# Chunk-selected attention and top-1 experts: head pairs in one written order for all engines, transposes in two visits, half the scores on two column tiles, bounds without the first query tile

## The chip, the cores and the metric

The kernel runs on one core of a Trainium2 chip. A core has five engines with instruction streams of their own: TensorE (PE; its weight loads are shown as PEld), VectorE (DVE), ScalarE (ACT), GpSimd (POOL) and SyncE (SP), which here only issues DMAs. They meet through semaphores, and each works its own stream in order. Matmuls write to PSUM[...]; DVE and ACT read PSUM[...]. The metric is device time in microseconds; the median of the runs before is 374.56.

## The reference

Attention over 4 batches, 8 heads, 768 positions and 64 columns per head, in which each query sees only 6 chunks of 32 keys, picked by an upper bound of its scores; then a mixture of 8 experts, of which each token takes one.

```python
ub = sum(maximum(q * k_min, q * k_max), axis=-1)      # per query and chunk of 32 keys
ub = where(causal, ub, -1e9)
top_chunks = argsort(ub)[..., -6:]
scores = where(sel & (pos_q >= pos_k), q @ k.T / 8, -1e9)
attn = exp(scores - max); attn = attn / (sum(attn) + 1e-9)
x = attn @ v                                          # 3072 tokens of 512
logits = x @ w_gate; e = argmax(logits); g = softmax(logits)[e]
out = g * (relu(x @ w1[e]) @ w2[e])
```

A query of the first 128 positions has at most four causal chunks, so its selection of six takes all of them.

## The kernel before

Work goes by pairs of heads: 16 pairs, four per batch (pair i: batch i // 4, `hp` = i % 4). The two heads fill the 128 partitions where both are needed, 64 each.

*Preparation of a pair* (`prep_steps`). `k_half` transposes three tiles of keys into a `ps_m` tile; DVE reduces it to largest and smallest value of each chunk, ACT copies the two heads, scaled by 1/8, to `KTE`. `q_t` and `q_e` do so for queries: DVE copies the transposed tile to `qT`, ACT writes its absolute value to `qA` and copies the second head to `QSB`; POOL copies the first head (in `late`, run by `flush`). `kse` forms sum and difference of largest and smallest on DVE, in `KS` and `KD`. `ub` multiplies them with `qT` and `qA`: q.(max + min) + |q|.(max - min) ranks chunks as the reference's bound does. ACT copies that to `ubT`, `select` transposes it, DVE adds the causal bias, finds the eight largest per row with MAX8 and marks every chunk below the sixth (`nsel`); `mask` transposes the marks, and ACT writes them as 24 further rows of `QSB`. `KTE` has -50 in the rows for each chunk's keys, so that the score matmul itself adds -50 for a chunk that is not selected.

*Attention of a pair.* Seven units of scores (`units`): units 0 and 1 for the first 384 queries, 2 to 6 for the second. `scores(i, u)` multiplies on TensorE (bf16, keys as columns of the array) into a `ps_s` tile, ACT takes Exp into `P`, POOL zeroes the part above the diagonal with affine_select where keys and queries meet (units 0, 1, 5, 6). `attend(i, u)` multiplies v with `P` (f32, the two heads on two column tiles of the array) into `po`, and DVE adds `P` to a running sum `acc`; at the end of a half DVE copies `po` to `ot`.

*Router steps of a pair* (`router_steps`). `ud` sums `acc` over the keys and multiplies `ot` with the gate on four column tiles; `lgp` transposes the result, DVE takes reciprocals and scales the logits, POOL adds them up (`sums`); `xr` transposes `ot` and writes the token rows to `xrow`. Per batch `route_steps` has `logits` (eleven DVE operations and an Exp on ACT), `rank` (counts on TensorE, five DVE operations) and `scatter` (POOL writes token rows to the expert's place in DRAM by indirect DMA, 128 rows each).

*Experts.* 31 tiles of 128 tokens at most, of which 28 run always: `gather`, `x_in` (a DMA transpose), `meta`, `up` (matmul, Relu, DMA transpose), `down` (matmul, scaling, indirect DMA to the output). Which expert a tile has is worked out by `table`, first for eleven tiles that three batches fill (19 DVE operations), then for the rest. The weights are loaded in 32 pieces by POOL (`load_w`), spread over the attention.

*Order.* TensorE, POOL and SP follow the order of the program. DVE and ACT do so in `first_pair` and from the last pair on; in between a scheduler places their instructions. The loop over pairs goes through four groups of units; with group g of pair i run the bounds and selection of pair i + 1, the keys and queries of pair i + 2, and router steps of pair i - 1. `first_pair` prepares pair 0 step by step, with spinning matmuls[...].

*Buffers.* PSUM: three banks in `ps_m` (transposes, bounds, masks, router), two tiles of two banks in `ps_s` (scores), one bank in `ps_o` (`po`).

Of the kernel before, what the change touches and what calls it, by code (L numbers as in the profile page):

```python
# [24 lines left out]
def kernel(  # L25
# [52 lines left out]
    cbias = const.tile([128, 3, 2, NCH], FP32)  # L78
    thr = const.tile([128, NT], FP32)
# [26 lines left out]
    def consts_first():  # L106
# [15 lines left out]
        nc.gpsimd.memset(nsel[:], 0.0)  # L122

    def consts_bias():
# [4 lines left out]
        for t in range(NT):  # L129
            nc.vector.tensor_scalar(thr[:, t:t + 1], chunk_p[:], float(4 * t), None, ALU.add)  # L130
# [4 lines left out]
    def consts_last():  # L135
        nc.gpsimd.memset(KS[1][:], 0.0)
        nc.gpsimd.memset(KD[1][:], 0.0)
        nc.gpsimd.memset(QSB[1][64:128], 0.0)
        nc.gpsimd.tensor_copy(out=KTE[1][64:128], in_=KTE[0][64:128])
# [18 lines left out]
    def load_w(s_):  # L158
        e, n = divmod(s_, 4)
        if n < 2:  # L160
            dst = w_all[:, ds(e * WE + n * 2 * F, 2 * F)].rearrange("p (c f) -> p c f", c=2)
            src = moe_w1[e, ds(n * 256, 256)]
        else:
            dst = w_all[:, ds(e * WE + W1W + (n - 2) * 4 * DM, 4 * DM)].rearrange("p (c f) -> p c f", c=4)
            src = moe_w2[e, ds((n - 2) * 512, 512)]
        nc.gpsimd.dma_start(out=dst, in_=src.rearrange("(c p) f -> p c f", p=128))  # L166

    late, sums_ = [], []

    def flush(*qs):  # L170
        for q_ in qs or (sums_, late):
            for f_ in q_:
                f_()
            q_.clear()
# [5 lines left out]
    def load(i, *names, eng=nc.sync):  # L180
        b, hp = divmod(i, HP)
        for nm, src in (("k", k), ("q", q), ("v", v)):
            if nm not in names:
                continue
            t_ = ld.tile([128, NT, 2, D], FP32, tag=nm, bufs=2 if nm == "v" else 1)
            for hd in range(2):
                eng.dma_start(out=t_[:, :, hd, :],
                                  in_=src[b, 2 * hp + hd].rearrange("(t p) d -> p t d", p=128))
            st[i][nm] = t_

    def prep_steps(i):
        s = st[i]
        kte, qsb, ks, kd = KTE[i % 2], QSB[i % 2], KS[i % 2], KD[i % 2]
        kmx = {}

        def k_half(hf):
            if hf == 0:
                s["kmx"] = work.tile([128, NCH], FP32, tag="kmx", name="kmx")
                s["kmn"] = work.tile([128, NCH], FP32, tag="kmn", name="kmn")
            pt = ps_m.tile([128, 384], FP32, tag="m")  # L200
            for t in range(3):
                nc.tensor.transpose(pt[:, ts(t, 128)], s["k"][:, 3 * hf + t], ident_f[:])  # L202
            pk = pt[:].rearrange("p (c w) -> p c w", w=CH)
            nc.vector.tensor_reduce(s["kmx"][:, ts(hf, 12)], pk, AX.X, ALU.max)  # L204
            nc.vector.tensor_reduce(s["kmn"][:, ts(hf, 12)], pk, AX.X, ALU.min)
            nc.scalar.activation(kte[0:64, 0, ts(hf, 384)], pt[0:64, :], AF.Copy, bias=0.0, scale=0.125)
            nc.scalar.activation(kte[0:64, 1, ts(hf, 384)], pt[64:128, :], AF.Copy, bias=0.0, scale=0.125)

        def q_t(hf):
            pt = ps_m.tile([128, 384], FP32, tag="m")  # L210
            for t in range(3):
                nc.tensor.transpose(pt[:, ts(t, 128)], s["q"][:, 3 * hf + t], ident_f[:])
            s[f"qp{hf}"] = pt

        def q_e(hf):
            pt = s[f"qp{hf}"]
            qT = work.tile([128, 384], FP32, tag=f"qT{hf}")
            qA = work.tile([128, 384], FP32, tag=f"qA{hf}")
            nc.vector.tensor_copy(out=qT[:], in_=pt[:])  # L219
            nc.scalar.activation(qA[:], pt[:], AF.Abs)  # L220
            late.append(lambda: nc.gpsimd.tensor_copy(out=qsb[0:64, 0, ts(hf, 384)], in_=qT[0:64, :]))  # L221
            nc.scalar.activation(qsb[0:64, 1, ts(hf, 384)], pt[64:128, :], AF.Copy)
            s[f"qT{hf}"], s[f"qA{hf}"] = qT, qA

        def kse():
            for hd in range(2):
                r = slice(64 * hd, 64 * hd + 64)
                c = slice(32 * hd, 32 * hd + NCH)
                nc.vector.tensor_tensor(ks[r, c], s["kmx"][r, :], s["kmn"][r, :], ALU.add)
                nc.vector.tensor_tensor(kd[r, c], s["kmx"][r, :], s["kmn"][r, :], ALU.subtract)  # L230

        def ub():
            pu = ps_m.tile([128, 384], FP32, tag="m")
            for w_, nm in ((ks, "qT"), (kd, "qA")):
                for hf in range(2):
                    nc.tensor.matmul(pu[64 * hf:64 * hf + 64, :], lhsT=w_[:], rhs=s[f"{nm}{hf}"][:],  # L236
                                     start=(nm == "qT"), stop=(nm == "qA"), skip_group_check=True)
            s["ubT"] = work.tile([128, 384], FP32, tag="ud", name="ubT")
            nc.scalar.activation(s["ubT"][:], pu[:], AF.Copy)
# [624 lines left out]
```

## Time and profile before

| | us |
|---|---|
| median of three runs | 374.56 (373.43 to 374.95) |
| the profiled execution | 363.95, its span on the core 362.1 |
| first scores of pair 0, pair 1 (all but one matmul from 32.83), pair 15 | 16.7, 31.3, 236.57 |
| first matmul of the experts | 248.8 |
| DVE's adds to `acc` (L325) | 81.5 busy, 112 times |
| ACT's Exp (L296) | 91.0 busy, 144 instructions |
| POOL's affine_selects (L300) | 38.4 busy, 96 times |

The attention fills the span up to about 245, the experts the rest. In what follows a row of the timeline has the start, the length to the end of its last instruction, the engine, the line, the operation, output and inputs, size, type and count. A row of a stretch has, after its length, the busy time of PE, PEld, DVE, ACT and POOL with instruction counts, TensorE's granted clock, the DMA engines' share and GB/s. A row of waits has the engine and line that waited, the one that released it, and the us in total, the number and the longest.

```profile
26.00:46.00 20.00, 17.64 (x130) 8.92 (x130) 17.61 (x56) 14.59 (x27) 8.29 (x16) 1.00 1.10 197
260.00:280.00 20.00, 20.00 (x105) 9.21 (x103) 8.71 (x56) 10.29 (x13) 12.88 (x13) 1.00 0.98 206
```

### The profile page before, as it was taken

To read this page: it belongs to the slowest core of one execution; us is meant where nothing else is said; L and a number is where in the kernel's file an instruction comes from. 1 tells how busy PE (TensorE), PEld (TensorE's weight loads), DVE (VectorE), ACT (ScalarE), POOL (GpSimd) and SP (SyncE) were. 2 spreads that over 40 slices of the span, in tenths; PEclk is the share of its full clock that TensorE was granted. 3 is DMA by queue.
4 is the path that set the end of the run, shared out by engine and by line. 5 is a ranking of instruction groups with operands and counts; after the bars stand their busy time and mean duration, and the time that the engine had idled before them with its cause. 6 is when DMAs were issued, how large, how long until landed. Compare 5 with 4: busy or idle time off the path is not lost. (4 is left out here: it accounts for less than half of the span.)

```text
span 362.1 us, 7547 instructions
## 1 busy us (share of the span) xinstructions
PE 335.4 (93%) x2312; PEld 173.4 (48%) x2312; DVE 232.1 (64%) x811; ACT 235.2 (65%) x398; POOL 177.1 (49%) x296
## 2 busy tenths in 40 slices
PE   6777999999999999999999997998999899999990
PEld 5534455465554554554545544443544344444440
DVE  5789788898998898998988999775370010000000
ACT  2496797797887977977879778462354445544450
POOL 3074333452476343457424538375576765555331
PEclk9999999999999999999999998999999999999996
DMA  7619997999948989957989992366999999999841
GB/s 148 114 24 198 201 206 113 217 194 177 219 108 185 191 121 195 205 123 193 167 138 201 183 186 67 83 125 121 164 193 236 204 245 211 215 197 193 175 123 51
DMA packets 138215, 59.83 MB, mean 165 GB/s; under 512 B 122811, under 2 KB 131005, under 8 KB 138176
## 3 DMA queue, kind: packets, MB, share of 16 engines
q1 hardware_dynamic: 119072, 29.52, 45.9%
q0 software_dynamic: 17536, 29.42, 42.0%
q10 hardware_dynamic: 1568, 0.39, 0.6%
q8 instruction: 21, 0.34, 0.4%
q14 instruction: 18, 0.15, 0.1%
HBM read 56.14 MB, written 10.51 MB: 184 GB/s over the span
## 5 line engine op out<-in xcount | busy, mean ns | idle before, releaser
L325 DVE TENSOR_TENSOR Pa<-Pa,Pr 128x768 f32<-128x768 f32 (+2 forms) x112 | 81.5, 728 | 1.8 <-DVE Pa L325 0.5
L300 POOL TENSOR_SCALAR_AFFINE_SELECT Pr<-Pr 128x256 f32<-128x256 f32 x80 | 31.9, 418 | 76.2 <-ACT Pr L296 75.3
L296 ACT ACTIVATE Pr<-ps 128x768 f32<-128x768 f32 (+2 forms) x112 | 65.0, 628 | 3.2 <-PE ps L291 2.9
L600 PE MATMUL py<-w_all,hT 128*128 x224 | 52.6, 379 | 1.0 <-DMA hT<-h__4066 0.8
L291 PE MATMUL ps<-QSB,KTE 128*128 128x384 bf16 (+2 forms) x288 | 49.1, 294 | 1.7 <-ACT QSB L265 1.2
L542 POOL DMA_INDIRECT xg<-xs_dram,grow x28 | 29.9, 1068 | 22.6 <-DVE gt_all L565 7.4
L563 DVE TENSOR_TENSOR ti_all<-xg,inv_i 128x1 int32<-128x1 int32 x17 | 2.8, 163 | 58.0 <-DMA xg<-xs_dram,grow 58.0
L291 PEld LDWEIGHTS <-KTE 128*128 128x128 bf16 x288 | 24.2, 98 | 32.6 <-issue 25.3
L608 POOL DMA_INDIRECT out_dram<-y,ti_all x28 | 27.8, 994 | 24.4 <-ACT y L607 18.7
L600 PEld LDWEIGHTS <-hT 128*128 128x128 bf16 x224 | 21.8, 98 | 27.6 <-DMA hT<-h__4066 1.2
L607 ACT ACTIVATE y<-py,gt_all 128x512 f32<-128x512 f32 x27 | 18.5, 687 | 20.6 <-PE py L600 19.9
L349 ACT ACTIVATE ud<-pu 128x384 f32<-128x384 f32 x16 | 7.9, 492 | 36.5 <-PE pu L346 36.5
L443 POOL DMA_INDIRECT xs_dram<-xrow,sli x24 | 26.9, 1121 | 6.6 <-issue 4.5
L589 PE MATMUL ph<-w_all,KTE 128*128 x120 | 28.4, 379 | 0.0
L296 ACT ACTIVATE Pa<-ps 128x768 f32<-128x768 f32 x32 | 26.0, 813 | 2.9 <-PE ps L291 2.3
L166 POOL DMA_DIRECT2D w_all<-in_moe_w_dram x32 | 24.4, 762 | 0.0
L300 POOL TENSOR_SCALAR_AFFINE_SELECT Pa<-Pa 128x256 f32<-128x256 f32 x16 | 6.5, 405 | 36.5 <-ACT Pa L296 36.5
L589 PE MATMUL ph<-w_all,QSB 128*128 x96 | 22.7, 379 | 0.2 <-issue 0.2
L379 DVE TENSOR_TENSOR xrow<-pt,rec 128x384 bf16<-128x384 f32 x32 | 17.6, 552 | 3.0 <-PE pu L236 1.7
L204 DVE TENSOR_REDUCE kmx<-pt 128x12 f32<-128x384 f32 x30 | 16.7, 556 | 4.0 <-PE pt L202 3.9
L221 POOL CAST QSB<-qT 64x384 bf16<-64x384 f32 x30 | 16.7, 564 | 4.1 <-DVE qT L219 2.7
L318 DVE COPY ot<-po 128x384 f32<-128x384 f32 x32 | 17.7, 553 | 1.2 <-PE po L313 1.2
(306 smaller groups left out, 639.5 us busy)
## 6 DMA issues: line engine op xcount, KB each, us to landing
w_all<-in_moe_w_dram POOLq DMA_DIRECT2D x32, 512.0 KB, 6.0
xg<-xs_dram,grow POOLq DMA_INDIRECT x28, 3.9
out_dram<-y,ti_all POOLq DMA_INDIRECT x28, 4.3
t__122<-in_k_dram SPq DMA_DIRECT2D x2, 192.0 KB, 3.5
t__125<-in_q_dram ACTq DMA_DIRECT2D x2, 192.0 KB, 4.0
t__128<-in_v_dram SPq DMA_DIRECT2D x2, 192.0 KB, 5.6
t__196<-in_k_dram SPq DMA_DIRECT2D x2, 192.0 KB
t__206<-in_q_dram SPq DMA_DIRECT2D x2, 192.0 KB, 3.7
```

The source lines that it names most:

```text
L166: nc.gpsimd.dma_start(out=dst, in_=src.rearrange("(c p) f -> p c f", p=128))
L291: nc.tensor.matmul(pv[:, hd, :], lhsT=kte[:, hd, ts(kb, 128)], rhs=qsb[:, hd, ds(qb * 384 + 384 - w, w)], start=True, stop=True, skip_grou ...
L296: nc.scalar.activation(P[:, :, ds(c0, w)], pv, AF.Exp)
L300: nc.gpsimd.affine_select(out=pd, in_=pd, pattern=[[0, 2], [1, 128]], compare_op=ALU.is_ge, fill=0.0, base=0, channel_multiplier=-1)
L318: nc.vector.tensor_copy(out=ot[:], in_=po[:])
L325: nc.vector.tensor_tensor(acc[:, :, 384 - w:384], acc[:, :, 384 - w:384], P[:, :, ds(c0, w)], ALU.add)
L443: d = nc.gpsimd.indirect_dma_start(out=xs_dram[:], out_offset=bass.IndirectOffsetOnAxis(ap=sli[:, u:u + 1], axis=0), in_=bst[b][f"xrow{u % ...
L542: d = nc.gpsimd.indirect_dma_start(out=xg_bufs[j % XB][:].bitcast(I32), out_offset=None, in_=xs_dram[:], in_offset=bass.IndirectOffsetOnAx ...
L589: nc.tensor.matmul(ph[:, fh, :], lhsT=xT[:, c, :], rhs=w_all[:, ds(wo + (c * F + fh * 512), 512)], start=(c == 0), stop=(c == NDC - 1), sk ...
L600: nc.tensor.matmul(py[:], lhsT=hT[:, c, :], rhs=w_all[:, ds(wo + (W1W + c * DM), DM)], start=(c == 0), stop=(c == NFC - 1))
L607: nc.scalar.activation(y[:], py[:], AF.Copy, bias=0.0, scale=fs[j]["gt"])
L608: d = nc.gpsimd.indirect_dma_start(out=out[:], out_offset=bass.IndirectOffsetOnAxis(ap=fs[j]["ti"], axis=0), in_=y[:], in_offset=None, bou ...
```

## The change

All five engines now follow the written order for the whole program. The groups are replaced by one function per pair:

```python
def iteration(i):
    p, n, m = i - 1, i + 1, i + 2
    b, hp = divmod(i, HP)
    last = i == NP - 1
    router = hp == 1 and b > 0
    rt = rout.get(p)
    for u in (0, 1):
        s_mm(i, u, i > 0)
        s_ex(i, u)
    if i > 1:
        rout[i - 2]["sums"]()
    if i == 0:
        k_prep(1, False); kse(1, nc.gpsimd); q_prep(1); q_c(1, 0); q_c(1, 1)
    else:
        av(p, 6)
        if not last:
            load(n, "v")
        o_ev(p, 1)
        add(p, 6)
        if router:
            route[b - 1][0]()
        if n < NP:
            ub_mm(n); ub_ev(n)
        if m < NP:
            q_prep(m)
        if n < NP:
            sel_mm(n); sel_v(n)
    if last:
        for j in range(XB):
            gather(j); x_in(j)
    if i == NP - 2:
        for _ in early_table:
            pass
    for u in (2, 3):
        s_mm(i, u); s_ex(i, u)
    if router:
        route[b - 1][1]()
    pieces(i, 2)
    av(i, 0); av(i, 1); add(i, 1); o_ev(i, 0)
    if i == 0:
        ub_mm(1); ub_ev(1)
    for u in (4, 5):
        s_mm(i, u, True); s_ex(i, u)
    pieces(i, 1)
    if router:
        route[b - 1][2]((0, 2, 4))
    if hp == 2 and b > 0:
        route[b - 1][2]((1, 3, 5))
    av(i, 2); av(i, 3); add(i, 3); add(i, 4)
    if i == 0:
        consts_last(); sel_mm(1); sel_v(1); q_prep(2)
    elif n < NP:
        mask_ev(n, mask_mm(n))
    if i > 0:
        rt["ud_mm"](); rt["ud_ev"]()
    s_mm(i, 6)
    if last:
        for j in range(XB, 2 * XB):
            meta(j - XB); gather(j)
            if j < len(x_slots):
                x_in(j)
    if m < NP:
        q_c(m, 0)
    s_ex(i, 6)
    if i == 0:
        av(i, 4); mask_ev(1, mask_mm(1))
    add(i, 5)
    if m < NP:
        k_prep(m, True); q_c(m, 1); kse(m, nc.gpsimd)
    if i > 0:
        rt["lgp_mm"](); rt["lgp_v"]()
        for hf in range(2):
            rt["x_mm"](hf)
        for hf in range(2):
            rt["x_v"](hf)
    if i > 0:
        av(i, 4)
    av(i, 5)
```

Each former step is cut into its TensorE part (`..._mm`) and the parts of other engines. In the diff, with what a sentence tells left out:

```diff
+    def q_c(i, hf):
+        for hd in range(2):
+            nc.gpsimd.tensor_copy(out=QSB[i % 2][0:64, hd, ts(hf, 384)],
+                                  in_=st[i]["qT"][64 * hd:64 * hd + 64, hf])
+    def q_prep(i):
+        q_mm(i, 0)
+        q_mm(i, 1)
...
+        q_T(i, 0)
+        q_A(i, 1)
+        q_T(i, 1)
+        q_A(i, 0)
+    def k_prep(i, two):
+        k_mm(i, two)
...
+        k_red(i, 0)
+        k_ev(i, 1)
+        k_red(i, 1)
+        k_ev(i, 0)
+    def s_mm(i, u, split=False):
...
+        for kb, w, c0 in parts:
+            for hd in range(2):
+                for h in range(2 if split else 1):
+                    n = 64 if split else 128
+                    nc.tensor.matmul(ps[ds(h * n, n), hd, ds(c0, w)], lhsT=kte[:, hd, ds(kb * 128 + h * n, n)],
+                                     rhs=qsb[:, hd, ds(qb * 384 + 384 - w, w)],
+                                     start=True, stop=True, skip_group_check=True)
+    def s_ex(i, u):
...
+        nc.scalar.activation(P[:], ps[:, :, 0:384], AF.Exp)
+    def o_ev(i, qb):
+        ot = work.tile([128, 384], FP32, tag="ot", bufs=3, name="ot")
+        if qb == 0:
+            nc.vector.tensor_copy(out=ot[:], in_=st[i]["po0"][:])
         else:
+            nc.scalar.activation(ot[:], st[i]["po1"][:], AF.Copy)
-                nc.tensor.matmul(pu[64 * hf:64 * hf + 64, :], lhsT=w_[:], rhs=s[f"{nm}{hf}"][:],
+                nc.tensor.matmul(pu[64 * h:64 * h + 64, 0:320], lhsT=w_[i % 2][:],
+                                 rhs=x_[:, ds(128 + 320 * h, 320)],
-        nc.gpsimd.dma_start(out=dst, in_=src.rearrange("(c p) f -> p c f", p=128))
+        nc.gpsimd.dma_start(out=dst, in_=src.rearrange("(c p) f -> p c f" if n < 2 else "(p c) f -> p c f", p=128))
-            nc.scalar.activation(h_[:], ph[:], AF.Relu)
+            nc.scalar.activation(h_[:].rearrange("q a (c p) -> q a c p", c=4),
+                                 ph[:].rearrange("q a (p c) -> q a c p", c=4), AF.Relu)
-        load(0, "k")
-        load(0, "q", eng=nc.scalar)
-        load(0, "v")
+        load(0, "k", (nc.sync, nc.scalar))
+        load(0, "q", (nc.sync, nc.scalar))
-        pm = ps_m.tile([64, S], BF16, tag="m")
+        pm = [mask_mm(0) for _ in range(2)]
```

So: key and query transposes of a pair stand in two places, not four; scores of units 0, 1, 4 and 5 go to two column tiles of 64 keys; a unit's Exp is one instruction; POOL writes both heads of `QSB` and, from `kse`, the sums and differences; ACT copies the second half's output. Bounds, selection and mask leave out queries 0 to 127 (the select's three transposes start at columns 0, 128 and 192 of 320). Key transposes go to a `ps_s` tile; the first half's `po` to a `ps_m` tile. In `first_pair` the two heads' loads go to two queues, v after the query transposes, and the mask is transposed twice, one tile for ACT and one for DVE; constants for the second buffer pair are set there. The weights' pieces start in `first_pair` with two; the pairs have 3, 3, 3, 3, 3, 0, 2, 2, 2, 0, 2, 2, 3, 0, 2 and none. Rows of w2 are laid out with four neighbours in a partition, and Relu writes the hidden columns in the matching order. After the last pair come its `av(15, 6)`, then `up(0)` and the rest as before.

## The prediction

> **What bounds the kernel now.** I read the page's first part, then the busy time by stretches, the waits, and the TensorE part of the timeline for one pair of heads. The first part names TensorE; a stretch in the middle of the attention shows that it is busy without a gap and that DVE and ACT stand little below it.
>
> ```profile
> PE 335.4 (93%) x2312; PEld 173.4 (48%) x2312; DVE 232.1 (64%) x811; ACT 235.2 (65%) x398; POOL 177.1 (49%) x296
> ```
> ```profile
> 106.00:126.00 20.00, 19.92 (x150) 10.42 (x146) 17.65 (x51) 17.18 (x32) 10.83 (x21) 1.00 0.99 193
> ```
>
> One pair lasts from 122.04 to 136.24, two starts of the same matmul group: 14.2 us, and most pairs repeat it to the hundredth. TensorE's rows of that pair, in part (start, length, and the tile: 128*128 uses the whole array, 128*64 two column tiles, 128*32 four):
>
> ```profile
> 122.04 0.87 PE L313 MATMUL po<-Pa,t__1683 128*64 128x384 f32 x4
> 122.74 0.82 PE L313 MATMUL po<-Pr,t__1683 128*64 128x256 f32 x8
> 123.39 0.81 PE L236 MATMUL pu<-qT,KS 128*64 128x384 f32 x4
> 124.03 0.81 PE L236 MATMUL pu<-qA,KD 128*64 128x384 f32 x4
> 124.78 0.85 PE L291 MATMUL ps<-QSB,KTE 128*128 128x384 bf16 x4
> 125.53 0.55 PE L244 MATMUL pt<-ident_f,ubT 128*128 128x128 f32 x3
> 126.00 0.87 PE L313 MATMUL po<-Pa,t__1683 128*64 128x384 f32 x4
> ...
> 127.44 0.85 PE L341 MATMUL pu<-Pa,dcol 128*32 128x384 f32 x8
> ...
> 128.87 0.50 PE L291 MATMUL ps<-QSB,KTE 128*128 128x256 bf16 x4
> ```
>
> Start to start, 123.39 to 124.03, four f32 records of 384 columns on two column tiles take 0.64; eight on four tiles take 0.67 (127.44 to 128.11). So tiles run side by side, and a group's price is its starts, not its length. The next group after a change of tile is late: 124.03 + 0.64 = 124.67, but the scores start at 124.78. I find 0.10 to 0.19 at each of nine such changes per pair, mean 0.13. The stream itself is scores 7 x 0.32 = 2.24, attention times v 7 x 0.64 = 4.48, bounds 1.28, sums and router 1.28, 24 f32 transposes x 0.107 = 2.57, six mask transposes 0.32: 12.17. With 9 x 0.13 = 1.17 that is 13.34; three waits close the rest to within 0.1:
>
> ```profile
> PEld pt L377 <- ACT KTE L207: 4.4, 12, 0.4
> PEld pt L377 <- ACT QSB L265: 4.1, 13, 0.3
> PEld pt L244 <- ACT ubT L239: 3.5, 12, 0.4
> ```
>
> [...] an ACT copy at L206 waits for DVE's L205 on the same tile (2.6 us over 15 waits). [...] L229 takes 0.16 alone and 0.48 beside a POOL cast.
>
> **The change, part by part.** All in us of the profiled execution (span 362.1; with launch 363.95).
>
> *TensorE in a plain pair.* Order after: scores 0, 1, attend 6, bounds (two tiles); query transposes, select transposes, scores 2, 3 (whole); attend 0, 1, scores 4, 5, attend 2, 3, mask (two); sums and router (four); scores 6, key transposes, router transposes, x transposes (whole); attend 4, 5. Five changes of mode instead of nine: -0.52. Bounds on 320 of 384 columns: -0.21. Split scores: each half streams the same columns on its own tile, side by side as L236 does; the doubled records may cost up to 0.1 at the 128-wide parts; taken 0.1. The three waits (0.95) go where transposes now lie between; but attend 0 needs a `ps_m` buffer that the later of ACT's two Abs frees: about 0.2. Sum 12.17 - 0.21 + 0.65 + 0.3 = 12.9.
>
> *ACT and DVE* shrink: ACT loses the second head's query copy (0.49 x 2), two small exponentials (0.17 x 2), some of the mask copy, and gains one output copy (0.49); DVE loses that copy (0.55) and the sums and differences of key bounds (17.4 / 16 = 1.1). From about 11.5 and 12.5 busy per pair to some 10.5 and 11. POOL gains two casts (2 x 0.5) and the four small operations; no row shows these on POOL. Nearest is L369, 0.65 for two of 128x48; I take 0.3 each, bounds 0.2 and 0.5.
>
> *What is late next: a ring through all engines.* The bounds of pair i+2 need those POOL operations, late in pair i. From one bounds start: 1.24 to the result, 0.6 its copy, 0.96 select and scores 2, 3, about 0.3 for the Abs, attend 0, 1 1.28, scores 4, 5 0.74, attend 2, 3 1.28, mask 0.32, change and sums 1.4: 8.1 with latency about 8.3. ACT's two mask copies (0.8 each) hold the next copy until 8.5; then that copy 0.5, exponential 6 0.85, key copies of one half 1.0, DVE's reductions of that half (ordered behind them by the shared tile) 1.0, POOL 1.2: 13.2. A plain pair therefore takes 13.2, bounds 12.7 (ring shorter than TensorE's sum) and 14.2 (POOL/DVE exclusion lengthens both).
>
> *Routing pairs.* Here the fixed order has a price. In the second pair of a batch POOL does the selects of scores 0, 1, then the logit sums, to 3.5; DVE starts `logits` only then, ACT's Exp of it at 4.1 stands ahead of the bounds copy (plain: 2.65), and DVE's two query copies stand behind all eleven `logits` operations (0.24 apart when dependent), at 5.75 instead of 3.05. Exponentials 2 and 3 and attend 0 follow: +2.85. Before, DVE's scheduler laid the same operations among others and the pair lost 0.4. Then come scatters, three together:
>
> ```profile
> 109.58 1.00 POOL L443 DMA_INDIRECT xs_dram<-xrow,sli  x1 [0.16 <-issue]
> 110.88 1.08 POOL L443 DMA_INDIRECT xs_dram<-xrow,sli  x1 [0.30 <-issue]
> ```
>
> Spacing 1.3, so 3.9; queued behind them are two query casts (1.0), the selects of scores 6 (0.8), two casts (1.0), key bounds (1.2), for which the next pair's bounds wait. In a plain pair this chain is just in time; behind scatters it ends some 1.75 late, bounds 0 and 2.5. That hits five pairs (after the second and third of a batch; the last has no bounds left). Pair 14 carries the early table's 19 DVE operations (19 x 0.24 = 4.5) ahead of the copy that frees a buffer, but no preparation: net +0.8.
>
> From pair 1's scores (32.83) to pair 15's (236.57) the kernel before takes 203.7. After: 14 x 13.2 = 184.8, + 3 x 2.85 + 5 x 1.75 + 0.8 = 202.9. That is -0.8.
>
> *Start.* Keys and queries on two queues ahead of v: about -0.7; two mask tiles let ACT and DVE copy side by side (DVE waited 1.45): -0.6. Pair 0 now holds pair 1's select behind constants whose last iota POOL reaches at about 12.4; that mask is ready 17.9 after the first scores instead of 15.5: +2.4. Sum +1.1, bounds -1.5 and +2.5.
>
> *Last pair.* Gathers 4 to 7 now stand on POOL before the selects of scores 6. Before:
>
> ```profile
> 245.56 1.13 POOL L300 TENSOR_SCALAR_AFFINE_SELECT Pr<-Pr 128x256 f32<-128x256 f32 x3
> 247.87 1.02 POOL L542 DMA_INDIRECT xg<-xs_dram,grow  x1 [1.18 <-DVE gt_all L565]
> 249.19 1.73 POOL L542 DMA_INDIRECT xg<-xs_dram,grow  x1 [0.30 <-DVE Pa L325]
> 252.99 1.02 POOL L542 DMA_INDIRECT xg<-xs_dram,grow  x1 [2.06 <-DVE Pa L325]
> 254.31 1.01 POOL L542 DMA_INDIRECT xg<-xs_dram,grow  x1 [0.30 <-issue]
> ```
>
> They wait for tables and row transposes and end 15.7 after gather 0 (239.59). TensorE needs those selects for attend 6, ahead of the first expert matmul; it is there about 10.7 after the pair's start, the selects between 16 and 20. First expert matmul: 17 to 21 instead of 12.2. The stall before `ud` at 250.6 to 254.3 (2.4 net) goes in return. Net +4, bounds 0 and +7.
>
> *At no cost:* second weights in (p c) rows and Relu's strided read. ACT is half busy in the expert stage (about 10 of 20 us); were Relu twice its 1.02, it would still lie under a tile's 3.45. Weight pieces sooner: the key, query and value loads have a pair of slack (landing 3.4 to 6.8), which is the cover.
>
> **Sum.** -0.8 + 1.1 + 4 = +4.3, about 366.4 of span. The median of the runs lies 10.6 above the profiled execution; I carry the difference over: 374.56 + 4.3 = 378.9.
>
> **Rivals.** (1) Faster: POOL's tail of scatters, casts and key bounds ends before TensorE reaches the bounds. Place: behind L443 in second and third pairs; price 5 x 1.75. It decides from about 12.9 per pair, when TensorE's own sum is the period. With the ring at 12.9 (-4.2), no late bounds (-8.75) and half the hole in the last pair (-2): 364; with routing pairs cheap too, 357. For it: TensorE has 1.3 less to do per pair. Against: the fixed order and POOL's five further pieces. (2) Column tiles of bf16 scores do not overlap: no row shows such a pair. Four split units then cost 0.32 more each, 1.28 x 15 = +19: 398. Against: f32 tiles overlap. (3) DVE becomes the bound through exclusion with POOL: 14.2 per pair, +14: 393. (4) Gains and losses cancel: 373 to 376.
>
> **Numbers.** Chances: forecast 0.42, rival 1 0.32, rival 2 0.05, rival 3 0.09, rival 4 0.12. Range 360 to 390 holds rival 1's upper part and most of the forecast's bounds; the forecast's own range is 376.5 to 387. No change is within 0.5%, 1.9 us. Faster 0.32, same 0.12, slower 0.56.
>
> **What would show it.** Score records as 128*64 at 0.32 to 0.42 per unit; five changes per pair; plain pairs at 13.2; query copies late by 2.7 in second pairs; LDWEIGHTS of the bounds waiting for POOL's key bounds after scatters; TensorE idle for 5 us or more before attend 6 of the last pair. The forecast is wrong if the bounds never wait for POOL, or if the last pair shows no hole.

## The result, and the profile after

The changed kernel takes 424.63 us (423.44 to 425.5, four runs) against 374.0 us before: a ratio of 1.137, with a 95% interval of 1.130 to 1.144. It is 51 us slower, where 4 were forecast. The profiled execution has a span of 421.6 us; that of the kernel before, 362.1. These two differ by 59.5 us and the medians by 51, since the profiled execution before was 10 us shorter than its median and the one after only 1; in which stage those 10 us lie isn't known. By the starts of each pair's scores (pair 1 of before at 32.83, as in the forecast) and of the first expert matmul (L615, L589 before), the 59.5 us split like this:

| stage, us | before | after | difference |
|---|---|---|---|
| to pair 0's scores | 16.7 | 16.2 | -0.5 |
| pair 0 | 16.1 | 19.3 | +3.2 |
| pair 1's scores to pair 15's | 203.7 | 252.9 | +49.2 |
| pair 15's scores to the first expert matmul | 12.2 | 18.8 | +6.6 |
| from there to the end | 113.3 | 114.4 | +1.1 |

The busy times of the page of after and its slices of granted clock, then the same slices before:

```profile
PE 353.4 (84%) x2468; PEld 198.4 (47%) x2468; DVE 226.7 (54%) x735; ACT 222.8 (53%) x352; POOL 217.7 (52%) x386
...
PEclk9896989889896969989797998869879999999999
```

```profile
PEclk9999999999999999999999998999999999999996
```

TensorE was busy for 335.4 us and is now for 353.4, though a pair has fewer mode changes and narrower bounds: the slices show why. The clock granted to it is under 0.9 of full speed in 16 of the 40 slices, down to 0.6. Before, it was 0.9 or more in all slices but two. Four pairs by stretches (start and end, length, then the busy time of PE, PEld, DVE, ACT and POOL with their instructions, the granted clock, the DMA share and GB/s): pairs 2 and 4, which are plain, pair 6, which follows a pair with scatters, and pair 8, plain again.

```profile
53.01:69.97 16.96, 14.74 (x120) 9.39 (x118) 12.23 (x33) 10.86 (x19) 8.39 (x19) 0.90 0.82 154
86.93:103.93 17.00, 14.74 (x120) 9.27 (x118) 12.27 (x33) 10.86 (x19) 8.42 (x20) 0.90 0.87 169
121.52:142.85 21.33, 16.17 (x120) 9.32 (x118) 12.41 (x34) 11.24 (x19) 11.58 (x22) 0.84 0.58 125
163.43:178.03 14.60, 13.07 (x120) 8.34 (x118) 12.15 (x33) 10.09 (x17) 8.36 (x18) 1.00 0.76 153
```

Pairs 2 and 8 run the same 120 matmuls, and one takes 2.4 us longer than the other: 1.7 us of that is longer TensorE work (14.74 against 13.07), at a clock of 0.90 against 1.00. But even pair 8, at full clock, is longer than the 14.2 of before. No engine is busy for the whole of it; something waits. From the waits of after (who waited on whom: us in total, times, longest):

```profile
ACT KTE L206 <- DVE kmn L202: 33.1, 27, 1.6
...
PE ps L298 <- ACT KTE L206: 28.7, 14, 2.7
...
PE po L327 <- POOL P L312: 10.7, 6, 6.1
POOL QSB L233 <- DMA xs_dram<-xrow,sli: 9.2, 5, 2.3
```

The first two belong together: ACT's key copies wait for DVE's reductions, and fourteen times, once per pair, TensorE's scores wait for those copies. The third holds the last pair's hole of 6.1 us, the fourth waits for scatters to land. The end of pair 2 and the start of pair 3 show the first two in the timeline (start, length, engine, line):

```profile
68.45 0.55 DVE L201 TENSOR_REDUCE kmx<-pk 128x12 f32<-128x384 f32 x1
...
68.92 0.54 DVE L202 TENSOR_REDUCE kmn<-pk 128x12 f32<-128x384 f32 x1
69.56 0.98 ACT L206 ACTIVATE KTE<-pk 64x384 bf16<-64x384 f32 x2 [1.61 <-DVE kmn L202]
69.97 0.49 PE L298 MATMUL ps<-QSB,KTE 128*64 128x384 bf16 x4
70.57 0.56 DVE L201 TENSOR_REDUCE kmx<-pk 128x12 f32<-128x384 f32 x1 [1.11 <-ACT KTE L206]
71.05 0.55 DVE L202 TENSOR_REDUCE kmn<-pk 128x12 f32<-128x384 f32 x1
...
71.63 0.98 ACT L206 ACTIVATE KTE<-pk 64x384 bf16<-64x384 f32 x2 [1.09 <-DVE kmn L202]
...
72.66 0.76 PE L298 MATMUL ps<-QSB,KTE 128*64 128x256 bf16 x8 [2.19 <-ACT KTE L206]
```

The order written out (`k_red(0)`, `k_ev(1)`, `k_red(1)`, `k_ev(0)`) was meant to have DVE on one half while ACT is on the other. But both halves lie in one `ps_s` tile, and the program orders DVE and ACT on the tile as a whole. So the four steps follow one another for 4.16 us (68.45 to 72.61), and since there are only two `ps_s` tiles, the scores of unit 1 (72.66) wait for the last of them: after those of unit 0 TensorE stands idle for 2.19 us.

### The profile page after: what moved, and what is told of

Its sections match the earlier page's. It is cut to its first block, busy times and chain, and to the rows that moved or that the text cites. A ratio compares the mean times of both kernels' runs of the same rounds, so it can differ in the third digit from the quotient of the medians.

```text
span 421.6 us, 7844 instructions
## 1 busy us (share of the span) xinstructions
PE 353.4 (84%) x2468; PEld 198.4 (47%) x2468; DVE 226.7 (54%) x735; ACT 222.8 (53%) x352; POOL 217.7 (52%) x386
## 5 line engine op out<-in xcount | busy, mean ns | idle before, releaser
L327 PE MATMUL po<-P,v_t 128*64 128x384 f32 (+2 forms) x576 | 94.2, 454 | 11.0 <-POOL P L312 10.7
L308 ACT ACTIVATE P<-ps 128x768 f32<-128x768 f32 x112 | 86.2, 812 | 19.3 <-PE ps L298 16.5
L335 DVE TENSOR_TENSOR P<-P 128x768 f32<-128x768 f32 (+2 forms) x112 | 87.8, 784 | 15.2 <-POOL P L312 6.6
L312 POOL TENSOR_SCALAR_AFFINE_SELECT P<-P 128x256 f32<-128x256 f32 x96 | 40.8, 443 | 101.7 <-ACT P L308 100.8
L298 PE MATMUL ps<-QSB,KTE 128*128 128x384 bf16 (+3 forms) x442 | 54.4, 309 | 28.7 <-ACT KTE L206 28.7
L327 PEld LDWEIGHTS po<-P,v_t 128*64 128x64 f32 x576 | 43.1, 149 | 44.3 <-issue 20.0
L298 PEld LDWEIGHTS <-KTE 128*128 128x128 bf16 (+1 forms) x442 | 32.1, 111 | 53.5 <-issue 46.8
L206 ACT ACTIVATE KTE<-pk 64x384 bf16<-64x384 f32 x64 | 31.0, 485 | 34.5 <-DVE kmn L202 33.1
L233 POOL CAST QSB<-qT 64x384 bf16<-64x384 f32 x60 | 41.6, 693 | 14.3 <-DMA xs_dram<-xrow,sli 9.2
L615 PE MATMUL ph<-w_all,KTE 128*128 x120 | 31.1, 399 | 3.9 <-issue 3.8
L634 ACT ACTIVATE y<-py,gt_all 128x512 f32<-128x512 f32 x27 | 18.5, 687 | 22.4 <-PE py L627 16.7
L201 DVE TENSOR_REDUCE kmx<-pk 128x12 f32<-128x384 f32 x32 | 17.7, 554 | 19.4 <-ACT KTE L206 15.8
L284 ACT ACTIVATE QSB<-pm 24x640 bf16<-24x640 bf16 x30 | 20.8, 692 | 5.2 <-PE pm L278 5.0
L615 PE MATMUL ph<-w_all,QSB 128*128 x96 | 22.7, 379 | 0.0
L615 PEld LDWEIGHTS <-KTE 128*128 128x128 bf16 x120 | 11.9, 100 | 20.3 <-issue 8.3
```

Source lines behind the costliest of these rows:

```text
L206: nc.scalar.activation(KTE[i % 2][0:64, hd, ts(hf, 384)], st[i]["pk"][hf][64 * hd:64 * hd + 64], AF.Copy, bias=0.0, scale=0.125)
L233: nc.gpsimd.tensor_copy(out=QSB[i % 2][0:64, hd, ts(hf, 384)], in_=st[i]["qT"][64 * hd:64 * hd + 64, hf])
L298: nc.tensor.matmul(ps[ds(h * n, n), hd, ds(c0, w)], lhsT=kte[:, hd, ds(kb * 128 + h * n, n)], rhs=qsb[:, hd, ds(qb * 384 + 384 - w, w)], s ...
L308: nc.scalar.activation(P[:], ps[:, :, 0:384], AF.Exp)
L312: nc.gpsimd.affine_select(out=pd, in_=pd, pattern=[[0, 2], [1, 128]], compare_op=ALU.is_ge, fill=0.0, base=0, channel_multiplier=-1)
L327: nc.tensor.matmul(po[64 * hd:64 * hd + 64, 384 - w:384], lhsT=vt[:, kb, hd, :], rhs=P[:, hd, ds(c0, w)], start=first, stop=last and n == ...
```

## The experiments

Each run is compared with the kernel before on its own chip, where that kernel's median lay between 363.7 and 374.0 us; so ratios are compared, not times. Lengths are from each run's profiled execution, first scores to first scores; half clock, the time at half speed, is 2 x (1 - mean clock) x span, as the records hold only 1.0 and 0.5. A profile shows one execution, and its half clock and its expert stage differ from one execution to the next (83 and 76 us, 114.4 and 118.2 us in two profiles of the changed kernel); so a difference of a few us between two profiles is weak evidence by itself.

| run | ratio (95%) | clock | half, us | pair 3 | pairs 5, 6, 7 | pair 15 to experts | pair 1 to 15 |
|---|---|---|---|---|---|---|---|
| before | 1 | 0.988 | 9 | 14.2 | 14.6, 14.2, 14.2 | 12.2 | 203.7 |
| after | 1.137 (1.130-1.144) | 0.902 | 83 | 17.0 | 17.6, 21.3, 20.6 | 18.8 | 252.9 |
| a0_same | 1.142 (1.134-1.149) | 0.910 | 76 | 15.3 | 17.8, 20.9, 20.5 | 19.5 | 252.0 |
| e1_two_tiles | 1.114 (1.108-1.120) | 0.928 | 58 | 13.7 | 16.3, 20.4, 20.5 | 20.8 | 235.2 |
| e2_warm | 1.131 (1.126-1.136) | 0.952 | 40 | 15.3 | 17.6, 20.4, 20.6 | 19.7 | 246.0 |
| e3_last | 1.129 (1.120-1.138) | 0.931 | 56 | 15.3 | 17.8, 21.1, 20.6 | 12.5 | 247.9 |
| e5_scatter | 1.122 (1.114-1.130) | 0.934 | 54 | 15.3 | 17.8, 19.3, 14.9 | 19.3 | 237.7 |
| e12_warm_all | 1.111 (1.107-1.115) | 0.991 | 7 | 15.3 | 17.6, 18.5, 19.3 | 22.3 | 241.1 |
| e6_three | 1.030 (1.022-1.038) | 0.972 | 21 | 13.7 | 17.5, 15.1, 15.7 | 12.8 | 213.6 |
| e7_logits | 1.041 (1.032-1.049) | 0.961 | 30 | 13.8 | 17.4, 17.7, 14.4 | 13.5 | 216.4 |
| e8_four | 1.056 (1.049-1.063) | 0.964 | 27 | 13.7 | 16.3, 21.0, 15.0 | 13.1 | 223.8 |
| e9_logits | 1.036 (1.029-1.042) | 0.973 | 20 | 13.7 | 15.9, 20.4, 14.5 | 12.8 | 216.3 |
| e10_unsplit | 1.064 (1.057-1.070) | 0.962 | 30 | 14.3 | 18.2, 20.7, 15.8 | 12.5 | 230.7 |
| e11_best | 1.024 (1.019-1.029) | 0.977 | 17 | 13.7 | 15.0, 19.1, 14.8 | 13.5 | 212.9 |

**Two key tiles.**

```diff
-            pk = ps_s.tile([128, 2, 512], FP32, tag="s", name="pk")
-            st[i]["pk"] = [pk[:, hf, 0:384] for hf in range(2)]
...
+            if two:
+                st[i]["pk"].append(ps_s.tile([128, 2, 512], FP32, tag="s", name="pk")[:, 0, 0:384])
```

> Edit: the two halves of the key transposes get a score tile each instead of one tile of two banks; nothing else. Theory A (one tile makes DVE's reductions and ACT's copies of the two halves follow one another, some 4.1 us instead of 2.1, and unit 1 of the next pair's scores waits 2.05 us for that buffer, 14 times; each such wait also brings a stretch of half TensorE clock): ACT's key copies no longer wait for the reductions of the other half (33.1 us to under 5), the wait of the scores for those copies goes from 28.7 to under 8 us, plain pairs from 17.0 to 13-14 us, the mean clock from 0.90 to over 0.96, and the time to 370-385 us. Rival B (the period is set by the chain over POOL: casts, selects, key bounds): the copies run side by side but plain pairs stay above 16 us and the time above 410. Rival C (waits go, the clock does not come back, its cause is elsewhere): about 424 - 28 = 396 us at a clock near 0.9.

The mechanism is as theory A has it. The timeline of this run, end of pair 4:

```profile
92.59 0.55 DVE L201 TENSOR_REDUCE kmx<-pk 128x12 f32<-128x384 f32 x1
92.68 1.99 ACT L206 ACTIVATE KTE<-pk 64x384 bf16<-64x384 f32 x4 [0.64 <-PE pk L185]
...
93.06 0.54 DVE L202 TENSOR_REDUCE kmn<-pk 128x12 f32<-128x384 f32 x1
...
93.69 0.56 DVE L201 TENSOR_REDUCE kmx<-pk 128x12 f32<-128x384 f32 x1
94.17 0.55 DVE L202 TENSOR_REDUCE kmn<-pk 128x12 f32<-128x384 f32 x1
...
94.89 0.82 PE L298 MATMUL ps<-QSB,KTE 128*64 128x384 bf16 x12
```

DVE and ACT run side by side and are done in 2.13 us instead of 4.16; twelve score records start without a wait. Plain pairs take 13.72 us and no half clock falls into them. Rival B is excluded, and so is rival C for these pairs. But the ratio falls by 0.023 to 0.028 only, 8 to 10 us of 370, and not by the 40 or more expected: pairs 6, 7, 10 and 11 stay at 20 us, and most of their half clock with them. This program spreads more than the others, from 399 to 412 us in five runs, so the size of the gain is known only roughly; even its fastest run is far above the 385 that was expected at most.

**Useless matmuls in one wait, then in all.** If the clock is lost because TensorE idles, it is kept by work of no use put into the idle time.

```diff
+            if u == 1 and i > 0:
+                for _ in range(24):
+                    nc.tensor.matmul(st[p]["po1"][0:64, 384:512], lhsT=ones_b[:, 0:64], rhs=ones_b[:],
+                                     start=False, stop=False, skip_group_check=True)
```

> Edit: 24 matmuls of no use (bf16, 64x128 into unused columns of a PSUM bank, some 1.3 us) put on TensorE in each of pairs 1 to 15 just ahead of unit 1's scores, that is into the wait for the key copies; the order of ACT and DVE on the shared tile stays. If the lost clock comes from that wait (theory A's second half): the mean clock rises from 0.90 to over 0.95 although the same wait stays, plain pairs fall from 17.0 to 15 us, and the time falls by 20 to 30 us to 395-405. If the clock has another cause: no gain, 424 us, or up to 15 x 1.3 = 20 us slower where the matmuls don't fit into the wait.

The clock rises to 0.952, but the ratio falls by 0.006 to 0.011 only, 2 to 4 us: the expected gain is missed. The same program without them, run again, tells why:

> No edit: the changed kernel again, as the yardstick on the chip of the three runs beside it. If the first comparison holds: 1.13 to 1.14 of the kernel before. If the lost clock hangs on where TensorE's idle spells fall against the windows of the clock (plain pairs of 15.3 us without and of 17.0 us with a stretch of half clock, both seen in the run with the last pair's selects moved): the number of such stretches differs from the first profile's while the waits of the scores for the key copies stay at 28-29 us, and the ratio may be anywhere in 1.11 to 1.14.

Its pairs 2 to 4 take 15.3 us at full clock as well, so against this run the useless matmuls had nothing to win there. Yet it is no faster than the first profile: the half clock is 76 us instead of 83, but pairs 1 and 13 are 1.6 and 1.7 us longer, and the stage from the first expert matmul to the end 3.8. The records of granted clock change only at the ends of stretches of 3.41 us; my reading is that whether a pair falls to half clock depends on how its idle spell lies against them. Each row below is one such stretch. First after, then the run with the last pair's selects moved, in the same columns as above:

```profile
52.32:55.73 3.41, 1.22 (x12) 0.51 (x10) 2.27 (x7) 2.00 (x5) 1.68 (x6) 1.00 0.83 177
55.73:59.15 3.42, 3.42 (x22) 2.40 (x23) 1.46 (x3) 2.05 (x3) 2.03 (x5) 0.50 0.06 14
...
69.39:72.80 3.41, 1.22 (x14) 0.56 (x12) 2.27 (x7) 2.11 (x5) 1.57 (x6) 1.00 0.94 197
72.80:76.22 3.42, 3.42 (x24) 2.24 (x20) 1.35 (x3) 1.94 (x3) 2.16 (x6) 0.50 0.21 48
```

```profile
51.34:54.75 3.41, 1.51 (x12) 0.63 (x9) 2.27 (x7) 1.71 (x4) 1.78 (x7) 1.00 1.10 231
54.75:58.17 3.42, 3.13 (x33) 2.31 (x33) 2.08 (x5) 2.61 (x6) 2.20 (x7) 1.00 0.44 97
...
82.06:85.47 3.41, 1.36 (x12) 0.52 (x9) 2.27 (x7) 1.82 (x4) 1.78 (x7) 1.00 1.14 223
85.47:88.89 3.42, 3.25 (x22) 2.42 (x23) 1.67 (x4) 2.24 (x4) 1.85 (x7) 0.50 0.40 88
```

PE busy for 1.22 or 1.36 us of 3.41 is followed by a stretch at 0.50; busy for 1.51, it is not. After's pairs 2 and 3 start 16.96 us apart, within 0.11 of five such stretches (17.07), so each idle spell meets nearly the same place of a stretch. This fits that pairs 2, 3 and 4 all fall in that profile and none of them in the other; no run tests it.

> Edit: the changed kernel with matmuls of no use put on TensorE ahead of its long waits: 24 before unit 1's scores (pairs 1 to 15), 24 before attend 6 and 24 before the bounds in the third and fourth pair of a batch, 24 before the select transposes of routing pairs, 60 before pair 1's mask in pair 0, 80 before attend 5 of the last pair; every wait of the changed kernel stays. Theory (a window of 3.41 us in which TensorE is busy for less than some 46% is followed by one at half clock, and most of these windows come from those waits): half clock falls from 76-83 us to under 30, the mean clock rises to over 0.96, and the ratio to the kernel before falls from 1.137-1.142 to 1.09-1.115, the share of the loss that is clock and not waiting. If the clock costs nothing because the waits decide anyway: half clock falls as far, the ratio stays above 1.125.

The view by cores of this run:

```profile
core 0: 411.4 us, clock 0.991
```

Half clock is gone but for 7 us, and the ratio falls from 1.137 or 1.142 to 1.111, by 0.025 to 0.031, as expected. So the clock is worth some 10 us of the 51. The useless matmuls cost something too (22.3 us instead of 18.8 to 19.5 from pair 15 to the experts), so 10 is a lower figure. An upper one, as an estimate, is half of the 69 to 75 us of half clock that went, 35 to 38 us, as a group of expert matmuls of 1.89 us took 3.58 at half clock; where between the two the clock lies isn't separated. At a clock of 0.991 the kernel is still 11% slower than before, and that is waiting, with what the useless matmuls cost.

**The last pair's selects ahead of the gathers.**

```diff
         s_mm(i, 6)
         if last:
+            s_ex(i, 6)
             for j in range(XB, 2 * XB):
```

> Edit: in the last pair the selects of scores 6 stand on POOL ahead of gathers 4 to 7 instead of behind them. Theory (forecast's step on the last pair): TensorE's wait of 6.1 us for those selects goes, the first expert matmul comes 12-14 us after the pair's start instead of 18.8, the time falls by 6 to 9 us to 416-419. Rival: the gathers then land later and the row transposes or the first expert matmul wait for them: less than 2 us gained.

POOL and TensorE of after at this place:

```profile
304.22 0.99 POOL L567 DMA_INDIRECT xgqA<-xs_dram,grow  x1 [0.30 <-issue]
305.22 0.78 POOL L312 TENSOR_SCALAR_AFFINE_SELECT P<-P 128x256 f32<-128x256 f32 x2
305.70 1.54 PE L327 MATMUL po<-P,v_t 128*64 128x256 f32 x8 [6.08 <-POOL P L312]
...
307.19 3.58 PE L615 MATMUL ph<-w_all,KTE 128*128 x8
```

The selects stand behind the eighth gather, attend 6 waits 6.08 us, and the first expert group runs at half clock (3.58 us; 1.89 in the run with the edit). With the edit the first expert matmul comes 12.5 us after the pair's start. In the profile this stage is 6.3 us shorter than in after and 7.0 shorter than in a0_same, and the stage behind it isn't longer (110.8 us instead of 114.4 and 118.2), which speaks against the rival. The ratio falls by 0.008 to 0.013, 3 to 5 us where 6 to 9 were expected, and the intervals of the ratios overlap: in the whole time the gain isn't clear of noise.

**The scatters.**

```diff
-        if router:
-            route[b - 1][2]((0, 2, 4))
-        if hp == 2 and b > 0:
-            route[b - 1][2]((1, 3, 5))
...
+        if router:
+            route[b - 1][2]((0, 2, 4))
+        if hp == 2 and b > 0:
+            route[b - 1][2]((1, 3, 5))
         for u in (4, 5):
             s_mm(i, u, True)
```

> Edit: the row scatters of each batch stand on POOL ahead of the select of scores 5, where POOL is idle for 3 to 7 us in the trace, instead of behind it and ahead of the query casts; nothing else. Theory (the scatters, 3.9 us of issue and some 2.2 us until they land, push casts, key bounds and so the next pair's bounds back): the pairs after a third pair (7 and 11) fall from 20.2-20.6 to 15-17 us, since nothing is waited for there; the pairs after a second one (6 and 10) fall by 1-3 us, as the row numbers come late; in all 9 to 14 us under the changed kernel. Rival (something other than the scatters makes those pairs long): pairs 7 and 11 stay within 1 us of 20.4.

What happens behind the scatters in after, POOL and TensorE:

```profile
121.08 0.98 POOL L467 DMA_INDIRECT xs_dram<-xrow,sli  x1 [0.30 <-issue]
...
122.04 0.53 POOL L233 CAST QSB<-qT 64x384 bf16<-64x384 f32 x1
...
124.83 0.50 POOL L233 CAST QSB<-qT 64x384 bf16<-64x384 f32 x1 [2.26 <-DMA xs_dram<-xrow,sli]
125.41 0.76 POOL L312 TENSOR_SCALAR_AFFINE_SELECT P<-P 128x256 f32<-128x256 f32 x2
125.86 0.87 PE L327 MATMUL po<-P,v_t 128*64 128x256 f32 x8 [1.32 <-POOL P L312]
...
127.80 0.23 POOL L214 TENSOR_TENSOR KS<-kmx,kmn 64x24 f32<-64x24 f32 x1
...
128.56 1.33 PE L242 MATMUL pu<-qT,KS 128*64 128x320 f32 x4 [1.83 <-POOL KS L214]
```

The second cast waits 2.26 us until the last scatter has landed (some 2.8 us from its end on POOL at 122.06), and the selects of scores 6, two more casts and the key bounds stand behind it; TensorE waits for both. The cast shares no tile with the scatters; yet in the trace it waits, until 124.83, on the very semaphores that tell of their landing. The first cast, just behind the last scatter, has no such wait. With the scatters moved, pair 7 falls from 20.5 to 14.9 us and pair 11 from 20.2 to 17.4; pairs 6 and 10 fall by 1.6 and 0.6. Of these falls, up to 3.4 us in pair 7 and up to 1.7 in pairs 6 and 11 can be half clock that went (6.8 and 3.4 us less of it). The ratio falls by 0.015 to 0.020, 6 to 7.5 us, less than the 9 to 14 expected. Its runs spread from 410 to 417 us, and the profile is of the fastest, so the profile shows more than the median does (8.9 us below a0_same on the same chip). A place behind the casts, the selects and the key bounds was planned too; it needs a fourth buffer for the rows, 52.6 KB per partition in a pool that has 49.7 (e4_scatter), so it has no time.

**Three together.**

> Edit: three together: two key tiles, the last pair's selects ahead of its gathers, the scatters ahead of the select of scores 5. If the three causes add up: plain pairs 13.7 us, pairs 7 and 11 at 14-16, the first expert matmul 12-14 us after the last pair's start, mean clock over 0.95, time 372-384 us, which is 1.02 to 1.055 of the kernel before. If they overlap (the slowest of several chains decides): over 390 us.

The ratio is 1.030, a fall of 0.107 to 0.112. Alone, the three give at most 0.028 + 0.013 + 0.020 = 0.061; taking the fastest run of each instead, they give 0.104 below a0_same, still short of the 0.112 of the three together. Pairs 6, 10 and 14 show where the rest is: against a0_same, two key tiles alone take 4.6 us off the three, the scatters alone 4.7, both (with the last pair's edit, which doesn't touch these pairs) 18.1. Half clock falls from 76 to 21 us. The likely reading is that two delays that end in the same wait hide one another, and that one of them is enough to keep TensorE idle for the greater part of a stretch; it is read from these lengths and not tested apart.

**The logits and the late constants.** On top of the three, the logits of a routing pair behind the query copies:

```diff
-            if router:
-                route[b - 1][0]()
...
                 q_prep(m)
+            if router:
+                route[b - 1][0]()
...
+        if router:
+            route[b - 1][1]()
         add(i, 1)
```

> Edit: as the three together, and in the second pair of a batch the logits' operations on DVE and ACT stand behind the query copies and the copy of the bounds, the ranks on TensorE behind attend 1. Theory (forecast's step on routing pairs, +2.85 each, seen as some 2.6 in pair 5 with two key tiles): pairs 5, 9 and 13 fall from 16.3-17.9 to 14-15 us, 5 to 9 us less in all than the three together. Rival: the row numbers then come later and the scatters push the next pair's bounds back by as much: pairs 5 and 6 together keep their sum, no gain.

The rival held: pair 5 stays at 17.4 us, pairs 5 and 6 take 35.1 together instead of 32.6, and the intervals of the two ratios overlap. In both, POOL stands still for up to 5.9 us for the row numbers, with the select of scores 5 behind it. So the next run leaves the second pair's scatters where the change had them, and moves the constants of pair 0:

```diff
         if i == 0:
-            consts_last()
             sel_mm(1)
...
+        else:
+            consts_last()
         av(i, 5)
```

> Edit: two key tiles and the last pair's selects ahead of its gathers as in the three together; the scatters ahead of the select of scores 5 only in the third pair of a batch, in the second at their old place; and in pair 0 the late constants at the end of the pair instead of ahead of pair 1's selection. Theory (each pair's length is set by its own late piece): pair 0 falls from 21.1 to 16-18 us and pair 1 from 16.1 to 13.7-14.5, pairs 5, 9, 13 from 17.5-18 to 16.3, while pairs 6, 10 stay at 15-17; 1.00 to 1.02 of the kernel before. If the scatters of the second pair cost the same wherever they stand on POOL: pairs 5 and 6 together stay at 32.6 us or rise.

Pairs 5, 9 and 13 fall to 16.3 us as expected, but the rest is a miss: the ratio is 1.056 where 1.00 to 1.02 was expected, and pairs 5 and 6 together rise to 37.2 us, so the scatters of the second pair cost more at their old place than POOL's wait for the row numbers does. Pair 0 falls only to 19.9: pair 1's mask comes 1.30 us late instead of 3.52, and then its first scores wait 2.07 us for the key copies behind the reductions.

> Edit: as the four together, and in the second pair of a batch the logits' operations behind the query copies and the copy of the bounds, the ranks behind attend 1. Theory (forecast's step on routing pairs): pairs 5, 9 and 13 fall by 1 to 2.5 us each against the four together, so 3 to 7 us in all, and may reach the kernel before. Rival (POOL's scatters, not DVE's logits, bound these pairs once the logits are out of the way): under 2 us in all.

Here the logits pay, 0.020 against e8_four, 7 us, at the upper end of what was expected, though the kernel before isn't reached. But the gain isn't where it was expected: pairs 5, 9 and 13 fall by only 0.4 to 0.6 each; pairs 6, 10 and 14 by 0.6, 1.4 and 3.3. The last of these loses its 6.8 us of half clock.

**Scores on the whole array.**

```diff
-            s_mm(i, u, i > 0)
+            s_mm(i, u)
...
-            s_mm(i, u, True)
+            s_mm(i, u)
```

> Edit: as the four together, but all scores on the whole array, as in the kernel before, instead of half of them on two column tiles. The forecast's step (each change of tile mode costs 0.13 us, and the split spares four of nine; its doubled records cost at most 0.1): plain pairs rise from 13.7 to 14.1-14.2 us, 5 to 7 us in all. Rival (mode changes lie beside waits for ACT and DVE that decide anyway): plain pairs stay at 13.7, under 2 us.

Against e8_four plain pairs rise from 13.72 to 14.26 us: 0.54 for four more mode changes, some 0.135 each, with what the doubled records of the split cost already taken off. In plain pairs the split scores of the change are worth a little more than they were priced at (4 x 0.13 less 0.1). From pair 1 to pair 15 the profile is 6.9 us longer, within the 5 to 7 expected, but 1.9 of that is pair 5 with a stretch of half clock; in the ratio it is 0.008, 3 us, with intervals that overlap.

**The best of these.** Both pairs with scatters get their key bounds from DVE:

```diff
+        busy = b > 0 and hp in (1, 2)
+        if not busy:
+            add(i, 5)
...
-            kse(m, nc.gpsimd)
+            kse(m, nc.vector if busy else nc.gpsimd)
...
+        if busy:
+            add(i, 5)
```

> Edit: two key tiles, the last pair's selects ahead of the gathers, all scatters ahead of the select of scores 5, the late constants at the end of pair 0, the logits behind the query copies; and in the second and third pair of a batch the key bounds' sums and differences on DVE instead of POOL, with the addition of scores 5 behind them. Theory (what is left in those pairs is POOL: casts that wait for the scatters to land stand ahead of the key bounds): pairs 5, 9, 13 fall from 17.4 to 15-16 us, 6, 10, 14 from 15-17.7 to 14-15.5, time 366-376 us on a chip where the kernel before takes 364-371, ratio 1.00 to 1.02. Rival (the selects of scores 6 behind the same landing hold attend 6): pairs 6 and 10 stay at 15.5-17, ratio 1.02 to 1.03.

Pairs 5, 9 and 13 take 15.0 us, as expected; pairs 6 and 10 take 19.1 and 18.0, above even the rival's figure. The timeline at the start of pair 6 in this run:

```profile
108.08 0.18 DVE L215 TENSOR_TENSOR KD<-kmx,kmn 64x24 f32<-64x24 f32 x1
...
110.42 0.50 POOL L233 CAST QSB<-qT 64x384 bf16<-64x384 f32 x1 [2.97 <-DMA xs_dram<-xrow,sli]
...
110.99 1.45 POOL L312 TENSOR_SCALAR_AFFINE_SELECT P<-P 128x256 f32<-128x256 f32 x2
...
112.13 1.55 PE L327 MATMUL po<-P,v_t 128*64 128x256 f32 x8 [3.46 <-POOL P L312]
```

The bounds' operands are ready at 108.26, but attend 6, ahead of the bounds on TensorE, waits 3.46 us for selects that stand behind the same landing. At 1.024 this version has the lowest ratio of those with the change, though the interval of e6_three overlaps with its own, and it is still slower than the kernel before. From pair 1 to pair 15 it takes 9.2 us more than the kernel before, and 8.0 of them are in pairs 6 and 10. No version with the change is faster than the kernel before.

## Why the prediction was wrong

The direction and the mechanics of TensorE were right; the size was wrong by more than ten times. Most of the loss lies in two steps of the sum that were priced too low, the ring and the scatters: with both mended, and the last pair's selects, the stretch from pair 1 to pair 15 takes 213.6 us (e6_three) instead of 252.9 or 252.0. A third, the clock, stood in no step.

- **TensorE's stream.** Confirmed. Score halves overlap (in pair 8 of after the eight records of two split units start at 170.82 and the next group at 171.47: 0.65 for two units, with 0.32 for each forecast), mode changes are five, and the price of one is some 0.135 where 0.13 was used. Rival 2 (column tiles don't overlap) is excluded. With two key tiles a plain pair takes 13.72 us; forecast were 13.2, within 12.7 to 14.2.
- **The ring, "key copies of one half 1.0, DVE's reductions of that half (ordered behind them by the shared tile) 1.0".** This is the step that failed first. I had seen that the tile orders the two engines, and applied it to one half. It orders all four steps: 4.16 us where 2.0 stood in the sum (whose terms, as written, add up to 13.05 and not 13.2). And I left out who else needs that buffer: unit 1's scores. A plain pair became 14.6 to 15.3 us at full clock and 17.0 with one stretch at half.
- **The clock.** In no step; it was put at nothing without a reason. The busy sum was made at full clock, as the trace of before shows it (0.988), and the waits were counted once; each one that leaves TensorE idle for the greater part of a stretch costs again in the stretch that follows (busy for 1.22 us of 3.41, then a stretch at 0.50). Measured by e12_warm_all: 10 us or more.
- **Scatters, "+1.75 in five pairs".** The mechanism was right (casts, selects, key bounds queued behind them), the term too small: it held only POOL's issue time, not the wait of a cast for the landing, 1.1 to 2.3 us in the five pairs of after. In e1_two_tiles, where the key tiles no longer add to it, pairs 6 and 7 are 6.7 us longer than a plain one. Their 6.8 us at half clock account for at most 3.4 of that. The four key-bound operations were priced at 0.3 each and take 0.23.
- **Logits, "+2.85" in pairs 5, 9 and 13.** Right for what it covers: some 2.6 us more than a plain pair in each of the three in e8_four, with no half clock in them, the query copy starting 5.4 us after the pair's start instead of 3.1 (e1_two_tiles, pairs 5 and 4).
- **Pair 14, "+0.8".** After has 20.3 us there, 10.2 of them at half clock. In e6_three the pair takes 13.6, so the early table itself costs nothing that shows.
- **Start.** Pair 1's mask was put at 17.9 us after the first scores, 2.4 later than before; pair 0 took 19.3 us, 3.2 more than before. The late piece is the one that was looked for, the mask of pair 1 behind the constants: its transposes wait 3.52 us for `nsel`. The stage up to pair 1's scores became 2.7 us longer, where 1.1 was forecast within -1.5 to +2.5.
- **The last pair.** Right: the hole before attend 6 was 6.08 us with "5 us or more" foretold, the first expert matmul came at 18.8 within "17 to 21". The stall before `ud` went as foretold. The rest of the stage was +1.1.

Rival 1 (faster) needed POOL to end before TensorE reaches the bounds; in after TensorE waited for the key bounds in all five scatter pairs, 1.1 to 1.8 us each. Rival 4 (gains and losses cancel) is out by the result. Rival 3 (DVE as the bound) is out: DVE is busy for 12.2 of 17 us.

## What to carry to other kernels

When two engines are meant to work on two halves at once, give each half a tile of its own: one tile that holds both is one thing to the program's order (4.16 us here, 2.13 with two tiles). When a wait is added, count how much of a fixed stretch TensorE stays busy, not only how long it waits; below some 40% the next stretch of 3.41 us ran at half speed here (72 of 73), and repairs made one at a time can look smaller than they are together. Behind a DMA on POOL's queue, look whether the next instructions wait for its landing (1.1 to 2.3 us in the five pairs of after), and add that to the sum and not the issue alone.

## What the runs showed of the hardware

The clock: the records of granted clock hold only 1.0 and 0.5, in stretches of 3.41 us or multiples, but for the last of each profile, which the end cuts off. In the fourteen profiles, from the fifth stretch of each on, 73 stretches at full clock had matmuls for less than 40% of the time; 72 of them were followed by half clock. From 40 to 48% it was 15 of 34, above 48% 6 of 1,277. The length of the longest idle spell within a stretch sorts them less well: of these 1,384 the best limit for it puts 42 on the wrong side, the best limit for the busy share 16. Useless matmuls in the idle time kept the clock up: 0.991 in e12_warm_all against 0.902 and 0.910. Idle spells of 2.19 us, as in the plain pairs of after, were enough to leave a stretch of 3.41 us busy for only 1.22 and the next at half clock.

The expert stage, which none of the experiments edits, takes 107.8 to 118.2 us from its first matmul to the end. In after, the eight matmuls of one group at L615 (1.89 us elsewhere) are spread over 6 us from 330.85, with nothing that the profile shows to wait for; other runs have such a stop at other places, or none. What causes it stays open.
